# Batch 0's keys with heads on the partition groups, turned by VectorE; the sketch matrices loaded from two queues and converted by VectorE alone

## The chip, the core and the metric

One of the eight cores of a Trainium2 chip runs the whole program. Its engines work side by side: PE (TensorE, matmuls and full transposes, results into PSUM), DVE (VectorE), ACT (ScalarE), POOL (GpSimd) and SP, which here only issues transfers. ACT can issue transfers too. The metric is the device time of one execution in microseconds (us); lower is better.

## What is computed

Two blocks in a row. The first is an attention with a polynomial sketch: q, k, v are 4 batches x 4 heads x 1088 tokens x 32 channels, S1 and S2 are 8 x 32.

```python
def phi(x):                       # 32 channels -> 64 features
    a = einsum('rd,bhsd->bhsr', S1, x)
    b = einsum('rd,bhsd->bhsr', S2, x)
    return einsum('bhsi,bhsj->bhsij', a, b).reshape(..., 64)
q_p, k_p = phi(q), phi(k)
kv  = einsum('bhsf,bhsd->bhfd', k_p, v);  z = sum(k_p, axis=2)
x   = (q_p @ kv) / (q_p . z + 1e-6)       # -> 4352 tokens x 128
h   = x @ w_in                            # 128 -> 2048
out = gelu(h) @ w_out                     # exact gelu, 2048 -> 128
```

q, k and v are float32. S1, S2, w_in and w_out arrive as float64, and the kernel rounds them to float32 itself from their two 32-bit words.

## The kernel before, in words

The 1088 tokens of a batch are 8 x 128 in the "main" part and 64 "rem". For batch 0 everything before the first product with w_in is a chain that nothing else can cover: keys and values must be summed into kv before any query can be answered. The engines take their instructions in the order in which the program's text issues them (lines 1218 to 1224 chain them), and a transfer queue likewise, so the order of the text is the order of the work. From the first `hidden` step on (line 1164) the program is a long software pipeline of matmuls with w_in and w_out, into which the attention of later batches is slotted.

What happens ahead of that pipeline for batch 0, with the names in the code:

- Loads (lines 187 to 200). ACT issues S1 and S2, then loads its table of functions. SP issues the keys in two transfers of two heads (`load_main`, line 99: token p*8+j lies on partition p, all heads side by side), one transfer of queries, the values in two transfers, two remainders of keys and one of values, w_in's first piece, the second queries, w_in's second piece.
- PE runs products of zeros (`keep_busy`, line 887) until keys and sketches are there.
- The sketches are rounded by the class `Rounding` (line 243): DVE takes exponent and mantissa bits, ACT converts the low word (`low_words`) and the exponent (`exponents`), DVE joins them (`mantissas`, `signs`, `product_for_heads`).
- Keys: `key_turn(0, 0)` transposes four 128x128 blocks on PE into one PSUM bank and ACT copies them out (`kT`); `sketches` transposes the sketch matrix on PE, DVE makes `S12` (masked by head) and `sT`, POOL repeats `sT` into `Srep`; `key_turn_apart(0, 1)` transposes four more key blocks, ACT copies in two halves.
- `query_turn(0)`: DVE turns the first queries in 32x32 blocks. `widen_v`: POOL copies values next to a column of ones.
- `key_features` (line 387): 32 products of 64x32 per head pair on PE (`key_products`), an ACT copy of one half, a DVE product over all pairs of features (`k_p`); one of four such products goes to POOL.
- `expand_products(0)` repeats the queries' sketches on PE, ACT copies, DVE multiplies (`q_pT`).
- `kv_first` (line 420) sums k_p times v over tokens on PE for head pair r = 0 and 1, with the remainder (`key_turn_rem`, `key_features_rem`, `kv_first_rem`) in between; ACT takes the sum (`kz`, line 930).
- Then the first numerators, the division, two turns, and the first products with w_in (`first_hidden`, line 737).

Batches 1 to 3 already use another layout for their keys: `load_keys` (line 103) puts head h on partitions 32h to 32h+31, 32 consecutive tokens to a partition, and `key_turn_blocks` (line 365) turns them by a single DVE instruction per half, in 32x32 blocks.

Of the kernel before, what the change touches and what calls it, by code (L numbers as in the profile page):

```python
# [8 lines left out]
FP = mybir.dt.float32  # L9
U32 = mybir.dt.uint32  # L10
AX = mybir.AluOpType
# [5 lines left out]
def kernel(  # L17
# [19 lines left out]
    B, H, S, D = q.shape  # L37
    R = S1.shape[0]
    F = R * R
# [31 lines left out]
    def work_bank():  # L71
        return work_banks()[:, 0]
# [23 lines left out]
    raw = {}  # L96
    src_of = {"q": q, "k": k, "v": v}

    def load_main(eng, n, b, heads=slice(0, H)):
        eng.dma_start(out=main[n, b][:, heads],  # L100
                      in_=src_of[n][b, heads, 0:MAIN, :].rearrange("h (p j) d -> p h j d", j=J))

    def load_keys(b):

        for h in range(H):
            sp.dma_start(out=main["k", b][h * 32:(h + 1) * 32].rearrange("t x j d -> t (x j d)"),
                         in_=k[b, h, 0:MAIN, :].rearrange("(t n) d -> t (n d)", t=32))

    def load_values(b):

        src = v[b, :, 0:MAIN, :].rearrange("h (t q n) d -> q t h (n d)", t=32, q=4)
        for g in range(4):
            sp.dma_start(out=main["v", b][g * 32:(g + 1) * 32].rearrange("t h n d -> t h (n d)"), in_=src[g])
# [14 lines left out]
                sp.dma_start(out=q_rem[h * 32:(h + 1) * 32, b % 2, b // 2],  # L128
                             in_=q[b, h, MAIN:S, :].rearrange("(n t) d -> t n d", t=32))

    def load_rem(n, b):
        sp.dma_start(out=rem[n][b // 2 * REM:(b // 2 + 1) * REM, b % 2],
                     in_=src_of[n][b, :, MAIN:S, :].rearrange("h p d -> p h d"))

    half_block = []
# [48 lines left out]

    S_dst = landing(SR, S1.dtype != FP)

    for i, s in enumerate((S1, S2)):
        s, e = words(s)
        act.dma_start(out=S_dst[i * R:(i + 1) * R, :], in_=s)
    nc.scalar.preload_act_table_set("gelu_and_others")  # L190
    for r in range(2):
        load_main(sp, "k", 0, slice(r, H, 2))
    load_q(0)
    for r in range(2):
        load_main(sp, "v", 0, slice(r, H, 2))
    for n, b in (("k", 0), ("k", 2), ("v", 0)):
        load_rem(n, b)
    load_w_in(0)
    load_q(1)
    load_w_in(1)  # L200
# [42 lines left out]
    class Rounding:  # L243
# [15 lines left out]
            if self.wide:  # L259
                act.activation(out=self.low, in_=self.lo, func=ACT.Copy, scale=2.0 ** -52)  # L260

        def fields(self):
            self.exponent_fields()
            self.mantissa_fields()

        def exponent_fields(self):
# [50 lines left out]
    def sketches():  # L317
        ps = work_bank()
        pe.transpose(ps[:, :2 * R], in_=SR_heads.rearrange("r h d -> r (h d)"), identity=ident[:2 * R, :2 * R])
        dve.tensor_mul(out=S12, in0=ps[:, None, :2 * R].broadcast_to([128, H, 2 * R]),  # L320
                       in1=mask4[:, :, None].broadcast_to([128, H, 2 * R]))
        dve.tensor_copy(out=sT, in_=ps[:, :2 * R])
        for i in range(2):
            src = sT[:, 0:R, None] if i == 0 else sT[:, None, R:2 * R]
            pool.tensor_copy(out=Srep[:, i], in_=src.broadcast_to([128, R, R]))

    def transposed(ps, name, srcs, copy, midway=lambda: None):

        n = len(srcs) * 128
        for i, s in enumerate(srcs):  # L330
            if 2 * i == len(srcs):
                midway()
            pe.transpose(ps[:, i * 128:(i + 1) * 128], in_=s, identity=ident)  # L333
# [4 lines left out]
    def four_tokens(n, b, h, c):  # L338
        return main[n, b][:, h, c * JC:(c + 1) * JC, :].rearrange("p j d -> p (j d)")


    kT, k_p, k_p_rem = {}, {}, {}

    def widen_v(r):
# [5 lines left out]
        rows = slice(b // 2 * REM, (b // 2 + 1) * REM)  # L350
        pool.tensor_copy(out=v_rem_aug[b][rows, :, 0:D], in_=rem["v"][rows, b % 2])

    def key_turn(b, r, ps, copy, midway=lambda: None):
        kT[r] = transposed(ps, "kT", [four_tokens("k", b, h, c) for h in (r, r + 2) for c in range(NCH)], copy, midway)

    def key_turn_apart(b, r, banks, copy):

        kT[r] = att.tile([128, CW], FP, name="kT")
        for h, ps in zip((r, r + 2), banks):
            for c in range(NCH):  # L360
                pe.transpose(ps[:, c * 128:(c + 1) * 128], in_=four_tokens("k", b, h, c), identity=ident)
        for i, ps in enumerate(banks):
            copy(out=kT[r][:, i * 256:(i + 1) * 256], in_=ps[:, :256])

    def key_turn_blocks(b, x):

# [9 lines left out]
    def key_products(r, banks, col=0):  # L376

        for i in range(2 * NCH):
            for c in range(2):
                for t in range(2):  # L380
                    at = i * 128 + c * 64
                    pe.matmul(banks[t][c * 64:(c + 1) * 64, col + i * 32:col + (i + 1) * 32],
                              lhsT=kT[r][t * 64:(t + 1) * 64, at:at + 64],
                              rhs=S12[t * 64:(t + 1) * 64, 2 * t:2 * t + 2].rearrange("p h r -> p (h r)"),
                              start=True, stop=True)

    def key_features(b, r, banks, by_pool=()):
        key_products(r, banks)

        k_p[b, r] = att.tile([128, 2, J, R, R], FP, name="k_p")  # L390
        a = att.tile([128, 2, J, 2 * R], FP, name="a_t")
        for t in (1, 0) if by_pool else (0, 1):
            ab = banks[t][:, :128].rearrange("p (n r) -> p n r", r=2 * R)
            if t in by_pool:
                act.copy(out=a[:, t], in_=ab)
                pool.tensor_mul(**spread(k_p[b, r][:, t], a[:, t, :, 0:R], a[:, t, :, R:2 * R]))
            else:
                act.copy(out=a[:, t, :, 0:R], in_=ab[:, :, 0:R])
                dve.tensor_mul(**spread(k_p[b, r][:, t], a[:, t, :, 0:R], ab[:, :, R:2 * R]))

    def key_turn_rem(pair, ps, copy):

        kT["rem"] = transposed(ps[:, 256:], "kT_rem", [rem["k"][:, pair].rearrange("p h d -> p (h d)")], copy)

    def key_features_rem(pair, ps):

        for rows in (slice(0, 64), slice(64, 128)) if pair == 0 else (slice(0, 128),):
            pe.matmul(ps[rows, 384:448], lhsT=kT["rem"][:, rows], rhs=S12.rearrange("p h r -> p (h r)"), start=True, stop=True)
        k_p_rem[pair] = big.tile([128, H, R, R], FP, name=f"k_p_rem{pair}")
        ab = ps[:, 384:448].rearrange("p (h r) -> p h r", r=2 * R)  # L410
        a = att.tile([128, H, R], FP, name="a_rem")
        act.copy(out=a, in_=ab[:, :, 0:R])
        dve.tensor_mul(**spread(k_p_rem[pair], a, ab[:, :, R:2 * R]))

    k_s = {}

    def flat(features):
        return features.rearrange("p i j -> p (i j)")

    def kv_first(ps, r, tokens=range(J)):  # L420

        for i in tokens:

            ch, t, one = i // 4, i // 2 % 2, i % 2
            for c in range(NP):
                pe.matmul(ps[c * F:(c + 1) * F, r * 2 * D:r * 2 * D + C], lhsT=flat(k_p[0, r][:, t, c * 4 + ch * 2 + one]),  # L426
                          rhs=v_aug[r][:, c, i, :C], start=(r == 0 and i == 0), stop=False, skip_group_check=True)

    def kv_first_rem(ps):
# [457 lines left out]
    def keep_busy(n, ps, cols=256):  # L887
        for i in range(n):
            noughts = [nc.const_aps.tensor(0.0, [128, m], FP) for m in (128, cols)]
            pe.matmul(ps[:, CW - cols:], lhsT=noughts[0], rhs=noughts[1], start=True, stop=True)  # L890
# [2 lines left out]
    keep_busy(3, bank)  # L893
    keep_busy(1, bank, 64)
    r = Rounding(SR)
    r.low_words()
    r.fields()
    r.exponents()
    r.mantissas()
    r.signs()  # L900
    r.product_for_heads(SR_heads)
    key_turn(0, 0, hidden_bank(), by_act)
    keep_busy(1, bank, 128)
    sketches()
    key_turn_apart(0, 1, [hidden_bank(), work_bank()], by_act)
    query_turn(0)
    widen_v(0)
    banks = [out_bank(), out_bank()]
    key_features(0, 0, banks)
    key_features(0, 1, [hidden_bank(), hidden_bank()], by_pool=(1,))  # L910
    widen_v(1)
    widen_v_rem(0)
    expand_products(0)
    for i in range(2):
        query_features(0, i)
    kv_bank = out_bank()
    kv_first(kv_bank, 0, (0, 1, 4, 5))
    key_turn_rem(0, banks[1], by_act)
    kv_first(kv_bank, 0, (2, 3, 6, 7))
    key_features_rem(0, banks[1])  # L920
    kv_first(kv_bank, 1)
    kv_first_rem(kv_bank)
    w_in = [Rounding(w) for w in w_in_sb[:2]]
# [74 lines left out]
    def add_tokens(b):  # L998
# [11 lines left out]
    held = {}  # L1010

    def sketch_and_attend(n):

# [241 lines left out]
```

## Time and profile before

| | |
|---|---|
| median of 3 runs | 259.32 us (258.89 to 259.87) |
| span of the profiled execution, first to last instruction | 258.0 us (its own whole time isn't listed beside the span) |
| difference of the two | 1.3 us |
| PE busy | 253.9 us (98%) |
| DVE, ACT, POOL busy | 151.0, 115.5, 163.5 us |
| first product with w_in (L737) on the chain | starts at 15.45 us |
| granted TensorE clock | 1.000 |

Times in a view are counted from the span's start. A group line gives line, engine, operation, written tile <- read tiles, shapes and count. Where a timeline row merges several instructions, its first number is the start of the first, its second the time from there to the end of the last. Matmuls are pipelined and their ends are modelled, so PE can look busy where it is partly waiting for one product's end.

### The profile page before, as it was taken

How to read it: one execution, taken by the hardware profiler on the slowest of the kernel's cores; microseconds unless marked ns; L12 is line 12 of the kernel's file. 1: busy time of each engine (PE TensorE's matmuls, PEld its weight loads, DVE VectorE, ACT ScalarE, POOL GpSimd, SP SyncE). 2: the span in 40 equal slices, each digit the busy share in tenths (PEclk: the TensorE clock that was granted, in tenths of full speed). 3: DMA queues.
4: the chain of work that ended last, by engine and by line, in shares of the span. 5: the costliest groups of instructions: out<-in, count | busy, mean ns of one | idle time of the engine just before them, and what ended most of it. 6: DMA issues, size and time to landing. Idle time of an engine off the chain costs nothing.

```text
span 258.0 us, 5769 instructions
## 1 busy us (share of the span) xinstructions
PE 253.9 (98%) x2335; PEld 136.1 (53%) x2335; DVE 151.0 (59%) x312; ACT 115.5 (45%) x224; POOL 163.5 (63%) x173
## 2 busy tenths in 40 slices
PE   8999999999999999999999999999999999999995
PEld 7856444345444545544444455455444444445794
DVE  2786888969699997590187986399307000700330
ACT  4685777443626332443335332533444334433442
POOL 3403006799968788487758775787758777877300
PEclk9999999999999999999999999999999999999999
DMA  6469848721000101102000002000200200020020
GB/s 199 144 185 374 188 95 217 213 76 14 3 0 12 31 1 21 23 6 37 3 0 3 0 9 38 0 1 3 41 3 4 39 0 1 7 36 0 3 41 20
DMA packets 29594, 13.48 MB, mean 52 GB/s; under 512 B 21888, under 2 KB 27776, under 8 KB 29568
## 3 DMA queue, kind: packets, MB, share of 16 engines
q1 hardware_dynamic: 29392, 13.05, 20.3%
q8 instruction: 18, 0.29, 0.5%
q10 hardware_dynamic: 176, 0.07, 0.1%
q14 instruction: 8, 0.07, 0.1%
HBM read 10.88 MB, written 2.23 MB: 51 GB/s over the span
## 4 chain that ended last, share of the span: by engine, by line
PE 98%; DVE 1%; issue 0%; ACT 0%; DVEq 0%
PE h_ps L721 45%; PE o_ps L807 33%; PE o_ps L858 5%; PE w_ps L855 3%; PE w_ps L437 1%; PE w_ps L890 1%; PE w_ps L578 1%; PE w_ps L633 1%; PE o_ps L426 1%; PE h_ps L737 1%; PE w_ps L978 1%; PE w_ps L656 0%; PE w_ps L543 0%; DVE x_tok L679 0%; PE h_ps L333 0%; PE w_ps L333 0%
## 5 line engine op out<-in xcount | busy, mean ns | idle before, releaser
L721 PE MATMUL h_ps<-xT,w_in 128*64 128x512 f32 (+3 forms) x514 | 136.9, 576 | 0.0
L728 ACT ACTIVATE block<-h_ps 128x512 f32<-128x512 f32 (+1 forms) x128 | 73.0, 571 | 117.3 <-PE h_ps L721 115.3
L721 PEld LDWEIGHTS h_ps<-xT,w_in 128*64 128x64 f32 (+1 forms) x514 | 41.9, 143 | 30.4 <-issue 11.6
L807 PE MATMUL o_ps<-block,w_out 128*64 128x256 f32 x224 | 57.5, 379 | 0.0
L772 POOL TENSOR_TENSOR bits_low<-block 128x512 f32<-128x512 f32 x28 | 35.9, 1281 | 27.8 <-ACT block L728 27.8
L807 PEld LDWEIGHTS o_ps<-block,w_out 128*64 128x64 f32 x224 | 30.5, 137 | 38.0 <-issue 27.5
L773 POOL TENSOR_TENSOR bits_a<-block 128x512 f32<-128x512 f32 x28 | 35.7, 1277 | 12.0 <-ACT block L728 11.9
L822 DVE COPY sums<-o_ps 64x256 f32<-64x256 f32 x8 | 3.3, 416 | 60.6 <-PE o_ps L807 60.6
L774 POOL TENSOR_TENSOR bits_e<-bits_a,block 128x512 f32<-128x512 f32 x28 | 36.0, 1286 | 2.2
L775 POOL TENSOR_TENSOR bits_m<-block,bits_e 128x512 f32<-128x512 f32 x28 | 35.8, 1279 | 2.2
L807 PE MATMUL o_ps<-bits_low,small 128*64 128x256 f32 x112 | 28.8, 380 | 0.0
L807 PE MATMUL o_ps<-bits_a,small 128*64 128x256 f32 x112 | 28.8, 380 | 0.0
L807 PE MATMUL o_ps<-block,small 128*64 128x256 f32 x112 | 28.8, 379 | 0.0
L807 PE MATMUL o_ps<-bits_m,w_out 128*64 128x256 f32 x112 | 28.8, 380 | 0.0
L807 PEld LDWEIGHTS o_ps<-block,small 128*64 128x64 f32 x112 | 15.2, 137 | 17.9 <-issue 10.8
L807 PE MATMUL o_ps<-bits_e,small 128*64 128x256 f32 x112 | 17.1, 383 | 0.0
L858 PE MATMUL o_ps<-g,w_out 128*128 128x512 f32 (+1 forms) x34 | 16.5, 572 | 0.0
L807 PEld LDWEIGHTS o_ps<-bits_m,w_out 128*64 128x64 f32 x112 | 15.4, 137 | 0.0
L807 PEld LDWEIGHTS o_ps<-bits_a,small 128*64 128x64 f32 x112 | 15.2, 137 | 0.0
L807 PEld LDWEIGHTS o_ps<-bits_low,small 128*64 128x64 f32 x112 | 15.2, 137 | 0.0
L590 DVE STREAM_TRANSPOSE w_ps<-w_ps 128x512 f32<-128x512 f32 (+1 forms) x7 | 4.8, 687 | 17.1 <-ACT xT L644 12.7
L807 PEld LDWEIGHTS o_ps<-bits_e,small 128*64 128x64 f32 x112 | 7.7, 137 | 10.6 <-issue 8.8
(194 smaller groups left out, 305.1 us busy)
## 6 DMA issues: line engine op xcount, KB each, us to landing
block<-in_moe_w_in_dram SPq DMA_DIRECT2D x3, 512.0 KB, 8.4
block<-in_moe_w_out_dram SPq DMA_DIRECT2D x3, 512.0 KB, 12.1
k<-in_k_dram SPq DMA_DIRECT2D x12, 128.0 KB, 3.1
v<-in_v_dram SPq DMA_DIRECT2D x12, 128.0 KB, 3.4
q<-in_q_dram SPq DMA_DIRECT2D x24, 64.0 KB, 2.4
out_dram<-oT SPq DMA_DIRECT2D x21, 64.0 KB, 2.2
k<-in_k_dram SPq DMA_DIRECT2D x2, 256.0 KB, 2.8
q<-in_q_dram SPq DMA_DIRECT2D x2, 256.0 KB, 3.9
```

Source lines behind the costliest of these rows:

```text
L426: pe.matmul(ps[c * F:(c + 1) * F, r * 2 * D:r * 2 * D + C], lhsT=flat(k_p[0, r][:, t, c * 4 + ch * 2 + one]), rhs=v_aug[r][:, c, i, :C], s ...
L590: dve.transpose(out=tok, in_=ps[:, :, :H2])
L721: pe.matmul(ps[rows, :W], lhsT=w[:, rows], rhs=xT[n][:, :W], start=True, stop=True)
L728: act.activation(out=g_of[n, fi][:, :W], in_=ps[:, :W], func=ACT.Gelu)
L772: pool.tensor_sub(out=s[3], in0=a11, in1=a21)
L773: pool.tensor_add(out=s[1], in0=a21, in1=a22)
L774: pool.tensor_sub(out=s[2], in0=s[1], in1=a11)
L775: pool.tensor_sub(out=s[4], in0=a12, in1=s[2])
L807: pe.matmul(acc[n][bank][half * 64:(half + 1) * 64, col:col + HW], lhsT=fixed, rhs=moving, start=opens and e == 0 and name in "4715", stop ...
L822: dve.tensor_copy(out=N[lo, 0, one], in_=a0[lo, one])
L855: pe.matmul(o_of[n][i][:, :128], lhsT=g[:, i * 128:(i + 1) * 128], rhs=w_tile(w_out_sb, fi), start=first, stop=final)
L858: pe.matmul(o_of[n][:, cols], lhsT=w_tile(w_out_sb, fi), rhs=g[:, cols], start=first, stop=final)
```

## The change

Batch 0's keys are loaded as those of the other batches: head h on partitions 32h to 32h+31. Heads 2 and 3 are issued by ACT, heads 0 and 1 by SP. S2 is the first transfer on SP, S1 stays the first on ACT. The two key remainders move to ACT's queue, behind its table load. The values are loaded in four transfers instead of two, 32 partitions each. The loads of w_in and of the second queries stay on SP in their order.

On the engines: the eight key transposes on PE and the three copies by ACT go. DVE turns the keys instead, by two instructions of 128x512 (`key_turn_first`). Both turns now come behind the sketches. The sketches' conversion runs on DVE alone: `fields(by_dve=True)` replaces the two ACT activations by three DVE instructions. `sT` is copied by ACT instead of DVE. The key products are as many as before (`key_products_first`), grouped by half of the tokens (x) instead of by head pair (r), so `kv_first` over the first four tokens needs half x = 0 of both banks, and over the last four half x = 1. `query_turn(0)` stands behind the first of the four feature products instead of ahead of them; POOL still makes one of these four products, between its two copies of values. One product of zeros of 256 columns stands behind the sketches, one of 128 behind the key products.

```diff
+    def load_keys(b, queue=sp, heads=range(H)):
+        for h in heads:
+            queue.dma_start(out=main["k", b][h * 32:(h + 1) * 32].rearrange("t x j d -> t (x j d)"),
+                            in_=k[b, h, 0:MAIN, :].rearrange("(t n) d -> t (n d)", t=32))
...
-    for i, s in enumerate((S1, S2)):
+    for i, (queue, s) in enumerate(((act, S1), (sp, S2))):
         s, e = words(s)
-        act.dma_start(out=S_dst[i * R:(i + 1) * R, :], in_=s)
+        queue.dma_start(out=S_dst[i * R:(i + 1) * R, :], in_=s)
+    load_keys(0, act, range(2, H))
     nc.scalar.preload_act_table_set("gelu_and_others")
-    for r in range(2):
-        load_main(sp, "k", 0, slice(r, H, 2))
+    for b in (0, 2):
+        load_rem("k", b, act)
+    load_keys(0, sp, range(2))
     load_q(0)
-    for r in range(2):
-        load_main(sp, "v", 0, slice(r, H, 2))
-    for n, b in (("k", 0), ("k", 2), ("v", 0)):
-        load_rem(n, b)
+    load_values(0)
+    load_rem("v", 0)
...
+            if by_dve and self.wide:
+                dve.tensor_scalar(out=self.m, in0=self.e, scalar1=2.0 ** 23, scalar2=-896.0 * 2.0 ** 23, op0=AX.mult,
+                                  op1=AX.add)
+                dve.tensor_scalar(out=self.r, in0=self.m, scalar1=0.0, scalar2=None, op0=AX.max)
+                dve.tensor_scalar(out=self.low, in0=self.lo, scalar1=2.0 ** -52, scalar2=None, op0=AX.mult)
...
-        dve.tensor_copy(out=sT, in_=ps[:, :2 * R])
+        act.copy(out=sT, in_=ps[:, :2 * R])
...
+    def key_turn_first(x):
+        kT[x] = att.tile([128, CW], FP, name="kT")
+        dve.transpose(out=kT[x].rearrange("p (j q t) -> p q j t", q=4, j=4),
+                      in_=main["k", 0].rearrange("p q j d -> p q (j d)")[:, :, x * 128:(x + 1) * 128].rearrange("p q (j d) -> p q j d", d=D))
...
+    def key_products_first(x, banks):
+        for t in range(2):
+            for j in range(4):
+                for c in range(2):
+                    at = x * 128 + j * 32
+                    pe.matmul(banks[t][c * 64:(c + 1) * 64, at:at + 32],
+                              lhsT=kT[x][t * 64:(t + 1) * 64, j * 128 + c * 64:j * 128 + (c + 1) * 64],
+                              rhs=S12[t * 64:(t + 1) * 64, 2 * t:2 * t + 2].rearrange("p h r -> p (h r)"),
+                              start=True, stop=True)
...
     keep_busy(3, bank)
     keep_busy(1, bank, 64)
     r = Rounding(SR)
-    r.low_words()
-    r.fields()
-    r.exponents()
+    r.fields(by_dve=True)
     r.mantissas()
     r.signs()
     r.product_for_heads(SR_heads)
-    key_turn(0, 0, hidden_bank(), by_act)
+    sketches()
+    keep_busy(1, bank)
+    banks = [hidden_bank(), hidden_bank()]
+    for x in range(2):
+        key_turn_first(x)
+    for x in range(2):
+        key_products_first(x, banks)
     keep_busy(1, bank, 128)
-    sketches()
-    key_turn_apart(0, 1, [hidden_bank(), work_bank()], by_act)
+    key_features_first(0, 0, banks[0])
     query_turn(0)
     widen_v(0)
-    banks = [out_bank(), out_bank()]
-    key_features(0, 0, banks)
-    key_features(0, 1, [hidden_bank(), hidden_bank()], by_pool=(1,))
+    key_features_first(0, 1, banks[1])
+    key_features_first(1, 1, banks[1], by_pool=True)
+    key_features_first(1, 0, banks[0])
     widen_v(1)
     widen_v_rem(0)
     expand_products(0)
...
-    kv_first(kv_bank, 0, (0, 1, 4, 5))
-    key_turn_rem(0, banks[1], by_act)
-    kv_first(kv_bank, 0, (2, 3, 6, 7))
-    key_features_rem(0, banks[1])
+    kv_first(kv_bank, 0, range(4))
+    key_turn_rem(0, rem_bank, by_act)
+    kv_first(kv_bank, 0, range(4, J))
+    key_features_rem(0, rem_bank)
     kv_first(kv_bank, 1)
     kv_first_rem(kv_bank)
```

More of the change, by code (lines that the diff above doesn't have):

```diff
@@ L97 @@
     src_of = {"q": q, "k": k, "v": v}
[L99 to L107, printed above, removed]
+    def load_keys(b, queue=sp, heads=range(H)):
+        for h in heads:
+            queue.dma_start(out=main["k", b][h * 32:(h + 1) * 32].rearrange("t x j d -> t (x j d)"),
+                            in_=k[b, h, 0:MAIN, :].rearrange("(t n) d -> t (n d)", t=32))
     def load_values(b):
@@ L129, in load_q_rem, with load_rem @@
                              in_=q[b, h, MAIN:S, :].rearrange("(n t) d -> t n d", t=32))
-    def load_rem(n, b):
-        sp.dma_start(out=rem[n][b // 2 * REM:(b // 2 + 1) * REM, b % 2],
+    def load_rem(n, b, queue=sp):
+        queue.dma_start(out=rem[n][b // 2 * REM:(b // 2 + 1) * REM, b % 2],
                      in_=src_of[n][b, :, MAIN:S, :].rearrange("h p d -> p h d"))
@@ L260, in low_words, with fields @@
                 act.activation(out=self.low, in_=self.lo, func=ACT.Copy, scale=2.0 ** -52)
-        def fields(self):
+        def fields(self, by_dve=False):
             self.exponent_fields()
+            if by_dve and self.wide:
[3 more added lines that the diff above has]
+                dve.tensor_scalar(out=self.low, in0=self.lo, scalar1=2.0 ** -52, scalar2=None, op0=AX.mult)
             self.mantissa_fields()
@@ L336, in transposed @@
         return t
-    def four_tokens(n, b, h, c):
-        return main[n, b][:, h, c * JC:(c + 1) * JC, :].rearrange("p j d -> p (j d)")
     kT, k_p, k_p_rem = {}, {}, {}
@@ L351, in widen_v_rem @@
         pool.tensor_copy(out=v_rem_aug[b][rows, :, 0:D], in_=rem["v"][rows, b % 2])
[L353 to L363, printed above, removed]
+    def key_turn_first(x):
+        kT[x] = att.tile([128, CW], FP, name="kT")
+        dve.transpose(out=kT[x].rearrange("p (j q t) -> p q j t", q=4, j=4),
+                      in_=main["k", 0].rearrange("p q j d -> p q (j d)")[:, :, x * 128:(x + 1) * 128].rearrange("p q (j d) -> p q j d", d=D))
     def key_turn_blocks(b, x):
@@ L374, in spread, with key_features_first @@
                     in1=b[:, :, None, :].broadcast_to([128, n, R, R]))
[L376 to L383, printed above, removed]
+    def key_products_first(x, banks):
[5 more added lines that the diff above has]
+                              lhsT=kT[x][t * 64:(t + 1) * 64, j * 128 + c * 64:j * 128 + (c + 1) * 64],
                               rhs=S12[t * 64:(t + 1) * 64, 2 * t:2 * t + 2].rearrange("p h r -> p (h r)"),
                               start=True, stop=True)
[L387 to L399, printed above, removed]
+        k_p[0, x] = att.tile([128, NP, J, R, R], FP, name="k_p")
+        held["a", x] = att.tile([128, NP, J, 2 * R], FP, name="a_t")
+    def key_features_first(x, t, ps, by_pool=False):
+        a, ab = held["a", x], ps[:, x * 128:(x + 1) * 128].rearrange("p (n r) -> p n r", r=2 * R)
+        if by_pool:
+            act.copy(out=a[:, t], in_=ab)
+            pool.tensor_mul(**spread(k_p[0, x][:, t], a[:, t, :, 0:R], a[:, t, :, R:2 * R]))
+        else:
+            act.copy(out=a[:, t, :, 0:R], in_=ab[:, :, 0:R])
+            dve.tensor_mul(**spread(k_p[0, x][:, t], a[:, t, :, 0:R], ab[:, :, R:2 * R]))
     def key_turn_rem(pair, ps, copy):
@@ L413, in key_features_rem @@
         dve.tensor_mul(**spread(k_p_rem[pair], a, ab[:, :, R:2 * R]))
-    k_s = {}
+    k_s, held = {}, {}
     def flat(features):
@@ L422, in kv_first @@
         for i in tokens:
-            ch, t, one = i // 4, i // 2 % 2, i % 2
             for c in range(NP):
-                pe.matmul(ps[c * F:(c + 1) * F, r * 2 * D:r * 2 * D + C], lhsT=flat(k_p[0, r][:, t, c * 4 + ch * 2 + one]),
+                pe.matmul(ps[c * F:(c + 1) * F, r * 2 * D:r * 2 * D + C], lhsT=flat(k_p[0, i // 4][:, c, i % 4 * 2 + r]),
                           rhs=v_aug[r][:, c, i, :C], start=(r == 0 and i == 0), stop=False, skip_group_check=True)
@@ L915 @@
         query_features(0, i)
-    kv_bank = out_bank()
-    kv_first(kv_bank, 0, (0, 1, 4, 5))
-    key_turn_rem(0, banks[1], by_act)
-    kv_first(kv_bank, 0, (2, 3, 6, 7))
-    key_features_rem(0, banks[1])
+    kv_bank, rem_bank = out_bank(), out_bank()
+    kv_first(kv_bank, 0, range(4))
+    key_turn_rem(0, rem_bank, by_act)
+    kv_first(kv_bank, 0, range(4, J))
+    key_features_rem(0, rem_bank)
     kv_first(kv_bank, 1)
@@ L1008, in add_tokens @@
         dve.tensor_add(out=to[rows], in0=sums[rows], in1=k_p_rem[b % 2][rows].rearrange("p (c r) i j -> p c (r i j)", c=NP))
-    held = {}
     def sketch_and_attend(n):
```

## The prediction

> **What bounds the kernel now.** The chain of waits comes first. PE holds 98% of it, and from 15.45 us on there is nothing in it but products; so a change in the opening is worth what it does to the start of that first product with w_in, one to one. Its shares, from the page, and its first pieces (start, us, what):
>
> ```profile
> PE 98%; DVE 1%; issue 0%; ACT 0%; DVEq 0%
> ```
>
> ```profile
> 0.77 3.22 PE w_ps L890 x8
> 4.00 0.85 PE h_ps L333 x4
> ...
> 6.54 0.78 PE o_ps L382 x32
> 7.32 0.47 PE h_ps L382 x32
> 7.78 1.05 PE w_ps L543 x32
> 8.83 0.59 PE o_ps L426 x16
> ...
> 10.50 0.91 PE o_ps L426 x32
> 11.41 0.35 PE o_ps L432 x8
> ...
> 15.45 1.06 PE h_ps L737 x8
> ```
>
> Two times matter: 8.83, where `kv_first` starts right behind `expand_products` (L543), and 11.76 (11.41 + 0.35), where kv is complete. Between them PE takes 2.93 us without a break.
>
> Second, the timeline of the same stretch shows who feeds PE (start, length, instruction):
>
> ```profile
> 3.63 0.17 DVE L268 TENSOR_SCALAR bits_e<-raw_SR 16x32 uint32<-16x32 uint32 x1 [2.67 <-DMA raw_SR<-in_S_dram]
> 4.46 0.28 DVE L302 TENSOR_TENSOR SR_heads<-bits_m,bits_e 16x128 f32<-16x128 f32 x1
> 5.21 0.28 PE L319 MATMUL w_ps<-ident,SR_heads 16*128 16x16 f32 x1
> 5.60 0.22 DVE L320 TENSOR_TENSOR S<-w_ps,mask 128x64 f32<-128x64 f32 x1 [0.86 <-PE w_ps L319]
> 5.92 0.71 DVE L528 STREAM_TRANSPOSE qT<-q 128x512 f32<-128x512 f32 x1
> 6.68 0.61 POOL L345 COPY sums<-v 128x512 f32<-128x512 f32 x1 [0.31 <-DMA v<-in_v_dram]
> 7.62 1.29 DVE L399 TENSOR_TENSOR k_p<-a_t,o_ps 128x512 f32<-128x512 f32 x2 [0.99 <-ACT a_t L398]
> 8.23 1.06 POOL L396 TENSOR_TENSOR k_p<-a_t 128x512 f32<-128x512 f32 x1 [0.94 <-ACT a_t L395]
> 9.24 0.61 POOL L345 COPY sums<-v 128x512 f32<-128x512 f32 x1
> 9.79 0.29 POOL L351 COPY v_rem_aug<-v_rem 64x128 f32<-64x128 f32 x1
> ```
>
> DVE has slack: it waits 0.86 and 0.99 us. PE has none, and spends part of it on key transposes. The sketches are ready at 4.74 (4.46 + 0.28), but PE reaches their transpose only at 5.21.
>
> Third, the groups by shape of 0 to 16 us: the same 128x128 transpose at about 4 us and at 11.7 us.
>
> ```profile
> L333 PE MATMUL h_ps<-ident,k 128*128 128x128 f32 x4 | 1.1, 421 | 0.0
> L333 PE MATMUL w_ps<-ident,q 128*128 128x128 f32 x4 | 0.7, 286 | 0.0
> ```
>
> 421 ns against 286: PE runs slow at first, though the granted clock reads 1.00 in every row. Counts in windows of 0.1 us put the step at about 6.65 us (6 products of L382 a window before 6.6, 17 to 22 after 6.9).
>
> **The change part by part.** The sum is against the profiled execution: span 258.0, 1.3 under the median of 259.32.
>
> *Sketches.* S2 is issued by ACT at 1.38 and lands at 3.62, 1.95 after its issue ended at 1.67. Now SP issues it at 0.73; with 0.45 per issue (row of the keys' loads) it lands near 3.1, and S1, whose issue ends at 1.35, near 3.3. Bounds: 2.4 (0.74 plus 1.7, the landing of the 8 KB q_rem transfers) and 3.6 (no gain). I take 3.2, from S2's own row. The conversion goes from 1.11 us (3.63 to 4.74) to eight DVE instructions in a line: 0.17 + 0.17 + 0.17 + 0.17 + 0.16 + 0.18 + 0.18 + 0.28 = 1.48, less some overlap where nothing depends: 1.4. So they are ready at 4.6 instead of 4.74. PE now transposes them at once; from PE's start to `S12` is 0.39 in the row, so `S12` runs 5.05 to 5.25 instead of 5.60 to 5.82: a gain of 0.55. `sT` on ACT costs the chain nothing: `Srep` needs 0.41 on POOL and is used after 8 us.
>
> *Keys.* Eight PE transposes (1.90 on the chain with their waits) and three ACT copies (0.58, 0.37, 0.37) go. In their place two DVE turns of 0.67 to 0.71 (rows L368, L528) follow `S12`: 5.2 to 6.6. They need all four key transfers. Before, 512 KB flowed by 3.65 and were there by 4.0. Two now go out behind S2 on SP, two behind S1 on ACT, the last by about 2.1; 2.7 from issue to landing (the row's least) gives 4.8, in time by 0.4. Upper bound 5.2 (3.1, the later 128 KB loads): still in time. The rearranged access of the new turn is not in the trace; bounds 0.67 and twice that, and I take 0.70 because the rows agree for any source so far. Products: half 0 from 5.95, half 1 from 6.65, done by 7.4 (0.85 and 0.65 as in the rows), against 7.78.
>
> *DVE's line.* Here the gain goes. Before, the queries' turn stood at 5.92, in DVE's idle time. Now the first feature product (0.65) and then the turn (0.70) follow the key turns: 6.7 to 7.35, and 8.05. `expand_products` waits for that turn: it starts at 8.1 instead of 7.78 and ends at 9.2 instead of 8.83. The other two feature products end at 8.7 and 9.35; `q_pT` waits for ACT's copy (0.59) as before and ends near 11.1 instead of 10.78, of which DVE's 0.54 of idle time before the denominators hides part. PE is 0.35 later.
>
> *Transfers.* SP's issues sum to about the same (S2 and two more value loads in, two remainders of 0.61 and 0.76 out). But a transfer waits for an earlier one to land once eight are in flight: in the built program the second value load waits for a key transfer of head 2, the third for head 3, the fourth for head 0. So three value loads go out at about 4.5 to 5.9, instead of 2.3 to 3.4 for both halves. A 128 KB value load lands in 2.4 (least) to 3.4 (median): 7.8 to 8.8; I take 8.2 as the queue is short then. w_in's first piece leaves near 6.5 instead of 5.49, the second queries near 7.0 instead of 6.14, w_in's second piece near 7.5 instead of 6.61. At 3.8 us each they land by 11.3, and are used at 10.63, 11.69 and 12.86: 10.3 for the first leaves 0.3. These I cost at nothing; without that slack each tenth would be one of the end. The key remainders leave ACT after its table load, near 3.6 to 4.9, and are used at 9.35; `sT` and the first `a_t` copy queue behind them on ACT, which is free by 5.
>
> *POOL's line.* The first copy of values waits for all four loads: 8.2 to 8.8 (before 6.68). Behind it wait the feature product (1.06, to 9.9), the second copy (10.5) and the remainder's (10.8). The second half of `kv_first`'s first round, due at 9.2 + 0.59 + 0.26 = 10.05, needs the product at 9.9: just in time. PE then ends kv at 12.15 instead of 11.76.
>
> *Sum:* 0.55 gained at the sketches and 0.38 at the products, none of which reaches PE's next stage, which starts 0.35 to 0.4 late: span 258.4, median 259.7.
>
> A rule against the change: the page "TensorE: Matmul & The Clock Gate" of the Trainium skill (Part 1, The HAM clock gate) says that the clock is halved until a free-running window of 3.4 us was busy. The trace agrees that it rises late, 5.9 us after the first product. By that page a window of the new opening that isn't busy enough would put the rise off by another 3.4 us, and the sum would be the first rival's 260.7; without it, it stands at 259.7.
>
> **The rivals.**
>
> - PE stays slow for longer (slower). Before, PE has work without a break from 0.77 to the step at 6.65. Now it stands idle about 4.0 to 4.6 for the sketches, 5.6 to 5.9 for the first key turn and 7.9 to 8.1 for the queries. For: PE was busy for 2.5 of the first 3.2 us and that did not bring the step. Against: two products of zeros fill most of the rest. While slow, the 1.05 of `expand_products` take twice as long, and the 2.93 of kv too. A step at 10 instead of 6.65 costs half of 8.1 to 10, 0.95, on top of 0.4: 260.7. It decides the sign of the verdict from a step at about 10 on. Range 260.3 to 262.
> - The values come late (slower). kv can't end before their landing plus 3.8 (0.61 + 1.06 + 0.59 + 0.23 + 0.91 + 0.35 and waits). At 9.2 instead of 8.2 that is 13.0, 1.2 late: 260.5. For: three loads wait for key landings. Against: little else is in flight then.
> - The rearranged turn takes twice 0.7: 1.4 later, 261.1. Against it speak six turns at 0.67 from another layout.
> - The sketches land at 2.4, the values at 7.6 (faster). `S12` is then bound by the zeros that end at 4.0, and kv ends at 11.4: 258.9. The 3.8 behind the values keeps it from being more.
>
> **How the numbers follow.** Likeliest, 0.45: PE's next stage 0.4 late, 259.7. Slow PE 0.25, late values 0.10, slow turn 0.05, early landing 0.15. A measurement of this kernel can tell about 0.5%, 1.3 us, from no change: 258.0 to 260.6. The likeliest case and the early landing lie within it; of the slow PE two thirds lie above it, of late values half, and the slow turn all, with some 0.05 from the likeliest case and the early landing running over: slower 0.32. Nothing worked out here reaches 258.0, so faster has 0.06, for what I have not seen. The range runs from 258.8, the early landing, to 261.2, two thirds into the slow PE.
>
> **What would show it.** Right: `S12` near 5.1, two turns of 0.7 behind it, PE waiting for the queries' turn near 8.1, kv complete near 12.1, w_in's products as before behind it. Wrong: transposes at 421 ns beyond 8 us; POOL's first copy of values after 9; a wait for w_in's pieces; or the queries' turn before 7.5, with which the opening would be shorter.

## The result, and the profile after

The changed kernel takes 267.16 us (266.37 to 267.63) against 259.31 us before: 1.029 times as long, with an interval of 1.028 to 1.031. The prediction was 259.7 us, with a range up to 261.2. PE's clock, which makes most of the difference, was on its list as a rise that comes late, with a chance of 0.25 and a price of 1 us. It cost about 5, and in the profiled run it was a fall.

The profiled run of the changed kernel took 266.37 us, with a span of 264.6: 6.6 longer than the span before. Two rows of its page, in 40 slices of 6.6 us each (PE's busy share and the granted TensorE clock, in tenths), and the shares of its chain of waits:

```profile
PE   6999999999999999999999999999999999999994
PEclk9559999999999999999999999999999999999999
...
PE 96%; DMA 1%; DVE 1%; ACTq 0%; ACT 0%; issue 0%; DVEq 0%
```

The two fives in the clock's row are new. In the second and third slice PE is busy nine tenths and more, at half speed. The windows of PE show where that begins and ends (columns: stretch, its length, PE's busy time and number of products, granted clock, DMA share, GB/s):

```profile
3.57:6.98 3.41, 2.07 (x54) 1.00 1.05 245
...
5.00:5.20 0.20, 0.00 (x0) 1.00 1.02 312
...
6.80:7.00 0.20, 0.20 (x22) 0.95 1.02 227
7.00:7.20 0.20, 0.20 (x18) 0.50 1.00 192
...
6.98:10.39 3.41, 2.88 (x52) 0.50 0.94 255
10.39:13.80 3.41, 3.41 (x57) 0.50 0.06 20
13.80:17.21 3.41, 3.41 (x58) 0.50 0.00 0
17.21:20.62 3.41, 3.41 (x95) 0.50 0.70 194
```

The clock falls at 6.98 and comes back at 20.62, 13.64 us later. That is four times 3.41, which is why the long stretches are cut in that length. In the stretch ahead of the fall PE was busy for 2.07 of 3.41, 61%; in the last three of the four slow ones it had no break at all.

It had been up before. The trace's own list of clock changes begins with a rise at 3.57, and the two zeros at 4.18 take 0.70, where the same two take 1.22 in a run below whose clock is first up at 13.54. In the kernel before, the first rise is listed at 6.91. So in this run the clock came up earlier than before, stayed up for one stretch of 3.41 and fell again.

The chain of waits up to the first product with w_in:

```profile
1.73 3.33 DMA k<-in_k_dram
5.26 0.72 DVE kT L353
6.02 1.41 PE h_ps L373 x54
7.70 0.69 DVE k_p L388
8.39 0.63 DVE qT L516
9.15 2.01 PE w_ps L531 x32
11.17 1.00 PE o_ps L414 x16
...
15.92 1.05 PE w_ps L334 x4
...
21.69 1.13 PE h_ps L725 x8
```

Set against the pieces shown of before, `expand_products` starts at 9.15 instead of 7.78, 1.37 later, and takes 2.01 instead of 1.05. The four transposes of the second queries (L334, 15.92) take 1.05 instead of the 0.59 that the chain before has for them at 11.76. The first product with w_in starts at 21.69 instead of 15.45, 6.24 later. Of that, 1.37 has come by the start of `expand_products`; the other 4.87 come between there and the first product (12.54 instead of 7.67), where PE's work is the same in number and shape and has no wait before it that it did not have. Behind 21.69 nothing more of size is lost.

Who feeds PE is seen in the timeline (start, length, instruction, and in brackets how long the engine had stood idle and for whom):

```profile
2.33 0.36 DVE L269 TENSOR_SCALAR bits_e<-raw_SR 16x32 uint32<-16x32 uint32 x1 [1.38 <-DMA raw_SR<-in_S_dram]
3.62 0.28 DVE L303 TENSOR_TENSOR SR_heads<-bits_m,bits_e 16x128 f32<-16x128 f32 x1
4.18 0.70 PE L878 MATMUL w_ps<-const-float32-0.0 128*128 128x256 f32 x2
5.26 1.31 DVE L353 STREAM_TRANSPOSE kT<-k 128x512 f32<-128x512 f32 x2 [0.68 <-DMA k<-in_k_dram]
6.02 1.88 PE L373 MATMUL h_ps<-S,kT 64*64 64x32 f32 x64 [1.15 <-DVE kT L353]
7.45 0.21 ACT L387 COPY a_t<-h_ps 128x64 f32<-128x64 f32 x1 [2.67 <-PE h_ps L373]
7.70 0.69 DVE L388 TENSOR_TENSOR k_p<-a_t,h_ps 128x512 f32<-128x512 f32 x1 [1.14 <-ACT a_t L387]
8.30 0.70 DVE L516 STREAM_TRANSPOSE qT<-q 128x512 f32<-128x512 f32 x1
8.92 0.61 POOL L342 COPY sums<-v 128x512 f32<-128x512 f32 x1 [3.66 <-DMA v<-in_v_dram]
9.15 2.01 PE L531 MATMUL w_ps<-qT,Srep 32*64 32x256 f32 x32 [0.53 <-DVE qT L516]
```

PE stands idle from 4.88 to 6.02, since the keys are there only at 5.26 and then have to go through DVE. Before, PE had no break here: zeros, the sketches' transpose and the key transposes that the change takes away follow one another from 4.00 to 6.54.

So the first theory: the idle place lets the clock fall, and the small products behind it don't bring it back. Its rival: the opening is simply longer, by the waits in the timeline (keys, the copy of `a_t`, the queries' turn, the values), and the slow products only fill time that something else sets.

### The profile page after: what moved, and what is told of

It is laid out like the page before. It is cut to its first block, busy times and chain, and to the rows that moved or that the text cites. A ratio compares the mean times of both kernels' runs of the same rounds, so it can differ in the third digit from the quotient of the medians.

```text
span 264.6 us, 5757 instructions
## 1 busy us (share of the span) xinstructions
PE 258.2 (98%) x2329; PEld 138.7 (52%) x2329; DVE 152.7 (58%) x316; ACT 113.9 (43%) x220; POOL 164.1 (62%) x173
## 4 chain that ended last, share of the span: by engine, by line
PE 96%; DMA 1%; DVE 1%; ACTq 0%; ACT 0%; issue 0%; DVEq 0%
PE h_ps L709 44%; PE o_ps L795 32%; PE o_ps L846 5%; PE w_ps L843 3%; PE w_ps L531 1%; PE w_ps L425 1%; PE o_ps L414 1%; PE w_ps L566 1%; PE w_ps L621 1%; DMA k<-in_k_dram 1%; PE h_ps L725 1%; PE w_ps L969 1%; PE h_ps L373 1%; PE w_ps L334 0%; PE w_ps L644 0%; PE h_ps L644 0%
```

## Experiments

Each kernel was timed beside the kernel before on the same chip; the medians of before lay between 259.3 and 259.5.

**Both idle places filled.** Products of zeros are added where PE stands idle; nothing else changes, so all waits stay.

```diff
     sketches()
-    keep_busy(1, bank)
+    keep_busy(3, bank)
...
-    keep_busy(1, bank, 128)
+    keep_busy(3, bank)
     key_features_first(0, 0, banks[0])
```

> The changed kernel with more products of zeros in PE's two idle places: three of 256 columns instead of one behind the sketches (the keys come at 6.0 us, PE sat idle from 4.88), and three of 256 columns instead of one of 128 behind the key products. Theory C (clock): the changed kernel lost 4.9 of its 6.6 us because PE's clock stood at half from 7.0 to 20.6 us, after a stretch from 3.6 to 7.0 in which PE had little to do; with the stretch filled the clock stays up, the granted clock reads 1.00 past 8 us with 128x128 transposes at 286 ns, and the time falls to 261 to 262.5 us. Theory W (waits): the time went to keys, queries and values that come later and to the new order, and the slow clock only stretches idle time; then more zeros can only delay PE, and the time stays at 267 us or above.

Measured: 261.67 us (261.26 to 261.89), 1.0074 [1.0052, 1.0095] times the kernel before. Five and a half of the lost microseconds come back for more work on PE. The granted clock reads 1.00 in all slices; the list of clock changes has a rise at 4.11 and no fall before 260.11. Its chain:

```profile
9.11 1.15 PE w_ps L531 x32
10.26 0.59 PE o_ps L414 x16
```

`expand_products` starts at 9.11, as late as in the changed kernel (9.15), and takes 1.15 instead of 2.01. From there to the first product with w_in, at 16.81, it is 7.70; before it was 7.67. The groups by shape of the opening say the same of single products. First the changed kernel's, then those of this run:

```profile
L531 PE MATMUL w_ps<-qT,Srep 32*64 32x256 f32 x64 | 4.0, 641 | 0.5 <-DVE qT L516 0.5
L414 PE MATMUL o_ps<-sums,k_p 128*64 128x33 f32 x64 | 4.0, 295 | 0.0
L334 PE MATMUL w_ps<-ident,q 128*128 128x128 f32 x4 | 1.1, 434 | 0.0
```

```profile
L531 PE MATMUL w_ps<-qT,Srep 32*64 32x256 f32 x64 | 2.3, 386 | 0.0
L414 PE MATMUL o_ps<-sums,k_p 128*64 128x33 f32 x64 | 2.4, 223 | 0.0
L334 PE MATMUL w_ps<-ident,q 128*128 128x128 f32 x4 | 0.7, 286 | 0.0
```

So the rival fails for the larger part: with the same waits the clock alone is worth 4.84 (12.54 less 7.70). The 1.33 by which `expand_products` still starts late (9.11 less 7.78) is left, and the waits have to explain only that.

**One place at a time.** The same fill in the first place alone, behind the sketches (the first hunk above), and in the second alone, behind the key products (the second hunk).

> The changed kernel with more products of zeros in the first idle place alone: three of 256 columns instead of one behind the sketches; behind the key products one of 128 as in the change. Theory C1: the idle 1.1 us ahead of the key products (4.9 to 6.0 us) is what brings the clock down, so filling it alone keeps the clock up: 261 to 262.5 us, as with both places filled. Theory C2: any idle PE in the opening does it, and the one ahead of the queries' products (8.6 to 9.1 at the slow clock, 7.8 to 9.1 at the full one) as well: 263 to 267 us, with the slow clock in the records past 10 us.

Measured: 261.59 us (261.47 to 261.72), 1.0079 [1.0052, 1.0105], with the clock at 1.00 throughout. The first place is enough.

> The changed kernel with more products of zeros in the second idle place alone: three of 256 columns instead of one of 128 behind the key products; behind the sketches one of 256 as in the change. Theory C1: the first idle place is left as it was, so the clock is down at 7 us as in the change; the zeros then take 2.6 us at the slow clock (to about 10), and they and the queries' products may bring the clock up near 10.4 us, or not before 14: 264 to 268 us. Theory C2: filling either place helps about equally: 262 to 264 us.

Measured: 263.79 us (262.88 to 264.87), 1.0164 [1.0114, 1.0214]: less slow than the first theory expected. The number lies in the range of the second, but either place does not help alike, since the first alone gives 261.59. The runs fall into two groups, 262.88 and 262.98 with a mean clock of 0.992, 264.61 and 264.87 with one of 1.00. The profiled run, of 264.87 us, has this chain:

```profile
6.40 2.45 PE h_ps L373 x64
8.85 2.86 PE w_ps L878 x6
11.70 2.00 PE w_ps L531 x32
13.70 0.59 PE o_ps L414 x16
```

The clock is down here: the zeros themselves take 2.86, nearly twice the 1.50 of the same six in the run with both places filled, and `expand_products` behind them takes 2.00. The list of clock changes has the first rise at 13.54, so in this run the clock was not up at all before. From 13.70 on the sums run at 0.59, while in the changed kernel they run at 1.00 from 11.17 to the end. The 3.41 ahead of the rise hold zeros up to 11.70 and `expand_products` from there; which of them brought the clock up is not shown. The 3.41 before those, full as well, with key products and 1.3 of zeros, ended without a rise.

**How full is full enough.** Two products of zeros behind the sketches instead of three or one.

```diff
     sketches()
-    keep_busy(1, bank)
+    keep_busy(2, bank)
```

> The changed kernel with two products of zeros of 256 columns behind the sketches instead of one (three kept the clock up); behind the key products one of 128 as in the change. Theory C1, by the share of a window: PE idles some 0.7 us ahead of the key products instead of 1.15. If what counts is how much of a window of about 3.4 us is filled, and the limit lies between one and three products, the runs fall into two groups, near 261.6 us (clock up) and near 265 to 267.5 us (clock down), by where the window begins. Rival: any idle place ahead of the key products brings the clock down; then all runs lie at 265 us or above.

Measured: 261.53, 261.38, 261.44 and once 266.45 us; two groups, as the first theory expected, and the last run has a mean clock of 0.974, as the profiled run of the changed kernel has. With the clock up the ratio is 1.0081 [1.0052, 1.0109]. One product of zeros was too little in all four runs of the changed kernel (266.4 to 267.6), two were enough in three of four, three in all fifteen runs of the two kernels above that have them there, and in all 26 of the four kernels below (at most 262.34).

The profiled run, of 261.53 us, has the clock up from 4.04 on. Two stretches of 3.41 behind that rise, in the same view as above, and a row of its timeline:

```profile
4.04:7.45 3.41, 2.53 (x67) 1.00 1.07 246
7.45:10.86 3.41, 2.35 (x61) 1.00 0.81 241
...
9.18 1.12 PE L531 MATMUL w_ps<-qT,Srep 32*64 32x256 f32 x32 [1.06 <-DVE qT L516]
```

In the second of them PE stands idle for 1.06 without a break, nearly the 1.15 of the changed kernel, and the clock stays up. So the length of one idle place doesn't decide alone. This stretch was busy to 69%, the one ahead of the fall in the changed kernel to 61%; whether the busy share is what counts, and where the limit lies, two such stretches can't show.

**Does the kernel before need its zeros as well?** Its five products of zeros are left out; the rest is as before.

```diff
     bank = work_bank()
-    keep_busy(3, bank)
-    keep_busy(1, bank, 64)
...
-    keep_busy(1, bank, 128)
     sketches()
```

> The kernel before without any product of zeros (five matmuls less, nothing else changed). Theory C: PE's first work is then the key transposes near 4 us, the clock rises at least one window of 3.4 us later and perhaps not before the dense products at 15 us, so the opening takes 3 to 6 us longer: 262 to 265 us. Theory W: nothing waits for those products, so the time stays at 259.3 us (within 0.5).

Measured: 260.56, 265.5, 264.9 and 266.23 us. Three of four runs lose 5 to 7 us, as the change does, with no key moved; the 19 runs of the kernel before beside them lie between 258.68 and 261.89. The fourth, which is the profiled one, has the key transposes and products running from 3.40 without a break, `expand_products` slow (1.94 from 7.63) and the sums nearly at speed from 9.57 (0.68). The list of clock changes has the rise at 9.74; the 3.41 ahead of it hold key products and `expand_products`. The other three were not traced; their time suggests that the clock came up later there. The kernel before, too, loses this time in most runs when its zeros are gone.

**Parts of the change alone.** First the sketches: S2 first on SP, the conversion by DVE, `sT` by ACT, in the kernel before.

```diff
-    for i, s in enumerate((S1, S2)):
+    for i, (queue, s) in enumerate(((act, S1), (sp, S2))):
...
-    r.low_words()
-    r.fields()
-    r.exponents()
+    r.fields(by_dve=True)
```

> The kernel before with the sketches' part of the change alone: S2 issued by SP, conversion on VectorE alone, sT copied by ACT; keys, values and queries as before. Theory C: PE's work stays as dense as before, so the clock rises as before and the time is 259.0 to 259.4 us, same. Theory W: the sketches land about 1.2 us earlier, but PE reaches them at 5.2 us in its order, so also same; a clearly slower run would put the loss into the sketches' part and would speak against both.

Measured: 259.48 us (259.26 to 261.44), 1.0008 [0.9979, 1.0037]. `expand_products` starts at 7.08, 0.6 earlier than before (7.71 in the same view), and yet the first product with w_in starts at 15.44 (before 15.45). The chain tells why:

```profile
5.86 0.60 SPq L173
6.46 0.04 issue
6.50 5.07 DMA q<-in_q_dram
```

The second queries, the last but one of the opening's loads on SP, land at 11.57, and their turn on PE follows at 11.71, against 11.76 before. A shorter opening runs into them.

Then the rest of the change, the keys with the values' loads and the new order, with the sketches as before (both issued by ACT, ACT in the conversion, `sT` by DVE):

```diff
-    for i, (queue, s) in enumerate(((act, S1), (sp, S2))):
+    for i, (queue, s) in enumerate(((act, S1), (act, S2))):
...
-        act.copy(out=sT, in_=ps[:, :2 * R])
+        dve.tensor_copy(out=sT, in_=ps[:, :2 * R])
...
-    r.fields(by_dve=True)
+    r.low_words()
+    r.fields()
+    r.exponents()
```

> The changed kernel with the sketches as before: both issued by ACT, low word and exponent converted by ACT, sT copied by VectorE; keys by heads on partition groups and turned by VectorE. Theory C: it is the keys' part that takes PE's work out of the opening, so the loss stays: 266 to 268.5 us, with the slow clock in the records or from the start. Theory W: the sketches are ready some 0.5 to 1 us later than in the changed kernel and the keys wait for them, so 267.5 to 268.5 us.

Measured: 268.78 us (268.61 to 269.07), 1.0346 [1.0295, 1.0398]. The loss comes with this part, and the sketches' part of the change saves 1.6 of it. The clock is up at 4.20 here and falls at 7.61, behind 3.41 in which PE was busy for only 0.84, and stays down for 17.07, five times 3.41. The keys are turned at 6.83 instead of 5.26, because the two that ACT issues, now behind both sketches, take 4.6 to land, against 2.5 for the two that SP issues; in the changed kernel it is 3.0 for either pair. In the view of the transfers issued up to 3.2 us (count, size, median us from issue to landing):

```profile
k<-in_k_dram SPq DMA_DIRECT2D x2, 128.0 KB, 2.5
...
k<-in_k_dram ACTq DMA_DIRECT2D x2, 128.0 KB, 4.6
```

**The waits that are left.** With the first place filled, the queries' turn goes ahead of the first feature product, and the zeros behind the key products go.

```diff
-    keep_busy(1, bank)
+    keep_busy(3, bank)
...
-    keep_busy(1, bank, 128)
-    key_features_first(0, 0, banks[0])
     query_turn(0)
+    key_features_first(0, 0, banks[0])
```

> The changed kernel with the first idle place filled (three products of zeros of 256 columns), the products of zeros behind the key products taken out, and the queries' turn on VectorE ahead of the first feature product instead of behind it. Theory Q: what is left of the loss with the clock up (261.7 against 259.5 us) is that the queries' products start at 9.1 instead of 7.8 us, because their turn stands behind a feature product that waits for the key products. Then they start near 7.7 us and the time is 259.5 to 260.5 us. Theory V: the values land at 8.8 us instead of 6.7, and what waits for them on GpSimd ends kv at 13.1 us anyway: 261 to 261.7 us.

Measured: 261.21 us (260.94 to 261.42), 1.0064 [1.0045, 1.0083]. `expand_products` starts at 7.68, as early as before the change (7.71 in the same view), but only 0.5 of the 1.4 gained there reaches the first product with w_in (16.30). The timeline shows what is late next:

```profile
7.68 1.12 PE L531 MATMUL w_ps<-qT,Srep 32*64 32x256 f32 x32
8.69 0.61 POOL L342 COPY sums<-v 128x512 f32<-128x512 f32 x1 [3.38 <-DMA v<-in_v_dram]
9.36 0.66 PE L414 MATMUL o_ps<-sums,k_p 128*64 128x33 f32 x16 [0.56 <-POOL sums L342]
```

PE stands idle for the values. They land at about 8.5 with the changed order of loads, and POOL's copy of them, which had been covered by the late `expand_products`, is now what the sums wait for.

Two more runs try to move the values. In the first, each half of the key products gets PSUM banks of its own, and the key remainders go back to SP, behind the values:

```diff
-    for b in (0, 2):
-        load_rem("k", b, act)
...
     load_values(0)
+    for b in (0, 2):
+        load_rem("k", b)
...
-    banks = [hidden_bank(), hidden_bank()]
+    banks, banks1 = [out_bank(), out_bank()], [hidden_bank(), hidden_bank()]
...
-        key_products_first(x, banks)
+        key_products_first(x, (banks, banks1)[x])
```

> As the kernel with the queries' turn ahead, and besides: the two key remainders back on SP behind the values (so the second to fourth value load no longer wait for key transfers to land, or only the last), and the key products of each half in PSUM banks of their own, so that ScalarE's first copy doesn't wait for the second half. Theory Q: little is left to gain by this, 259.3 to 260.3 us, and no faster than the kernel with the queries ahead by more than 0.3. Theory V: the values then land near 7.9 us, and this is the step that brings the time down: 0.7 to 1.2 us faster than that kernel, to about 259.5 to 260.5 us.

Measured: 260.96 us (260.65 to 261.35), 1.0047 [1.0019, 1.0075]. The copy of `a_t` now starts 0.70 after the first key product (7.36 against 6.66), where it was 1.29 in the run with the queries first, with the clock up as well (7.53 against 6.24): it waits for one half only. POOL's copy of the values comes at 8.53 and the sums at 9.20, a little earlier, but the second queries, issued behind the remainders, now set the chain: their turn on PE starts at 12.69, and the first product with w_in at 16.41.

The second adds to this that ACT issues half of the values, and that the value remainder goes behind the second queries:

```diff
+    load_values(0, act, range(2, 4))
     load_keys(0, sp, range(2))
     load_q(0)
-    load_values(0)
+    load_values(0, sp, range(2))
...
-    load_rem("v", 0)
     load_w_in(0)
     load_q(1)
+    load_rem("v", 0)
```

> As the kernel with the queries' turn ahead, the first idle place filled and the key products in banks of their own (261.0 us), and besides the values' four loads issued two by ACT behind its table load and two by SP, so that only the last waits for a key transfer; the key remainders follow on SP, the values' remainder goes behind the second queries. Theory V: what is left of the loss is the values, copied by GpSimd from 8.5 us on instead of 6.7; they now land 0.5 to 1 us earlier, kv is complete near 11.7 us, and the time is 259.9 to 260.6 us. Theory D: VectorE's line (two key turns, the queries' turn, three feature products, done at 9.5 us) holds kv back by itself, and the time stays at 260.8 to 261.2 us.

Measured: 260.75 us (260.73 to 260.83), 1.0055 [1.0038, 1.0072], the first product with w_in at 16.12. The second queries are no longer late, but the values are as late as ever, although all four loads left earlier (2.34 to 4.21, against 2.49 to 5.30 in the run with the queries first):

```profile
8.69 0.62 POOL L343 COPY sums<-v 128x512 f32<-128x512 f32 x1 [3.37 <-DMA v<-in_v_dram]
```

The last of them, in the chain of the run with the queries first and then of this one (start, us):

```profile
5.30 3.19 DMA v<-in_v_dram
```

```profile
4.21 4.27 DMA v<-in_v_dram
```

It leaves 1.09 earlier and lands at the same 8.48 or 8.49. The prediction had the wait of the value loads for key loads as a reason for late values; here leaving earlier did not bring the last load in earlier.

One more run asks whether it is the split over two queues that brings the keys so late: all four go out on SP.

```diff
-    load_keys(0, act, range(2, H))
...
-    load_keys(0, sp, range(2))
+    load_keys(0, sp)
```

> The kernel with the first idle place filled and the queries' turn ahead, with all four key transfers on SP, ahead of queries and values, instead of two on SP and two on ACT. Theory S (sharing): with keys on ACT and queries and values on SP, the second queue's transfers run beside the keys and take half the engines; on one queue the keys go first. Then the last key transfer, though issued 0.7 us later (near 2.5), lands by about 4.8 to 5.1 instead of 5.4, the key turn starts there, and the time is within 0.5 us of the 261.2 of that kernel or better. Theory I (issue): the landing follows the issue, so the keys land near 5.8 to 6.0 and the time is 261.5 to 262 us.

Measured: 261.32 us (261.08 to 262.34), 1.0085 [1.0058, 1.0112], beside 261.21 for the same kernel with the keys on two queues. The keys are turned at 5.59, between the two expectations. Each load takes less (2.7 us in the median, against 2.9 for SP's and 3.1 for those of ACT on two queues), but the last one leaves later, at 2.49. The time lies in the range of the first theory, the turn does not; neither theory of the landing is shown by this.

None of these versions is faster than the kernel before; the best, at 260.75, is still 0.55% slower.

## Why the prediction was wrong

- **The clock: the step that failed.** The sum took PE's products at the durations that they have before, with one rise of the clock near 6.65 (6.91 in the trace's list) and no fall, and priced a later rise as a rival: "A step at 10 instead of 6.65 costs half of 8.1 to 10, 0.95". In the profiled run the clock rose at 3.57, fell at 6.98 and was back only at 20.62, and the cost was 4.87 (or 4.84 between two runs that differ by zeros alone). So the rival named the right part, but not its course: a fall behind a rise was not among the rivals. Two more things in this step were wrong. "Two products of zeros fill most of the rest" against the rival: the one behind the sketches took 0.70 of a place that lasts from 4.18 to 6.02. And the rival took it for granted that a clock that is down rises at the end of the next full stretch. In the trace two of them, busy from end to end, ended with the clock still at 0.50, and only the end of the third brought it up. With that the rival's range ended at 262. The sign that the prediction named for a slow PE came, a transpose of 421 ns beyond 8 us: at 15.92 it is 434.
- **What I had from the skill.** The page "TensorE: Matmul & The Clock Gate" of the Trainium skill (Part 1, The HAM clock gate) has a free-running window of 3.4 us. The trace agrees: 13.64 us of slow clock are four of 3.41, and the fall lies at the end of one that was busy to 61%. It has the clock come up after one busy window; here it did not after two full ones of small products, at 10.39 to 17.21, and "another 3.4 us", as I had it by that page, was too little.
- **Sketches.** Forecast to land at 3.2; they were there at 2.33, just under the lower bound of 2.4. The conversion took 1.57 (2.33 to 3.90), forecast 1.4. So the gain at this step was larger than my 0.55, and of no use: the keys were not there.
- **Keys.** Forecast to be there at 4.8, upper bound 5.2. The turn began at 5.26, released by the last key transfer. I called the upper bound "still in time", which held only beside my own late sketches. The two turns took 0.72 and 0.6 (1.31 together), as forecast, so the rival of a slow turn is out.
- **Key features.** Forecast at 6.7, came at 7.70. I let the first copy follow the products of the first half. It came only behind those of both halves, which share a bank; with banks of their own (the run with four banks) it follows the first half. With the late keys that makes 1.0 that the sum does not have.
- **The queries' turn.** That it would make `expand_products` wait was right, with the turn at 8.3 (forecast 7.35) and PE at 9.15 (forecast 8.1), later by the missing 1.0. This is the second term that was too small: `expand_products` was put 0.35 to 0.4 late and is 1.37 late. With the clock up and nothing else changed it is 1.33, and the time of 261.6 to 261.7 still lies above the range.
- **Values.** Forecast at 8.2, came at 8.92 in POOL's row. So late values were there too, but hidden behind the late `expand_products`. It shows only where that comes earlier (0.56 of PE's idle time in the run with the queries first).
- **Later transfers at nothing.** Right for the changed kernel: neither w_in nor the second queries are on its chain. The sketches alone and the four banks show how thin the cover is: the second queries become the chain as soon as `expand_products` starts 0.6 earlier.
- **Behind the opening.** Right: from the first product with w_in on, the delay stays as it is, 6.24 there and 6.6 at the end of the span.

The sum of what was measured against the profiled runs: 1.37 of waits, 4.87 of clock, 0.4 behind 21.69 that I have not traced: 6.6 of span. A comparison of medians gives 7.85, since the profiled run of the changed kernel is the fastest of its four and its span is 1.8 below its time, while in the base of the prediction I had 1.3 for that difference. In other runs of the kernel before it is 1.8 as well, so the profiled execution of before was some 0.5 longer than its median. The two runs of the changed kernel at 267.6 us have a mean clock of 1.000, so no fall is on record for them. That fits a clock that first came up late, as the rival had it: the record counts as 1.00 what lies ahead of the first rise, and the profiled run with the second place filled reads 0.999 although its clock is first up at 13.54. For the runs at 267.6 this is argued from their time and mean, not traced.

Left open: why POOL can copy the values only at 8.5 to 8.9 in most of these orders of loads (at 9.10 with the sketches as before, at 9.32 with all keys on SP), also where ACT issues half of them, while the DMA engines are close to fully used from 2.5 to 9 us (a share of 0.82 to 1.17 in the changed kernel); and what in PE's work raises the clock or leaves it down. The full stretches that ended without a rise in the changed kernel hold mostly sums; the four traced rises that come late (9.74 without zeros, 13.54 with the second place filled, 20.62 in the changed kernel, 24.68 with the sketches as before) each end a stretch with 1.7 to 2.0 of `expand_products` in it. But in the last of these runs a stretch with 2.0 of it, busy to 91%, ended without a rise.

## What to carry to other kernels

Work taken off PE in a stretch where the clock is not yet safely up has to be priced by what the clock then does to everything behind it, and not only by the wait: here a stretch with an idle place of 1.15 us cost 4.9. When a change empties PE, put products of zeros into the hole and see how many it takes over several runs, as here two products were enough in three runs of four and three in all. A mean clock of 1.00 doesn't tell that the clock was up in the opening; the length of a known product does. And before moving transfers, look at which one is next in line on the chain: a gain of 0.6 at the start of an opening was lost to the second queries, and 1.4 shrank to 0.5 by the values.

## What the runs showed of the hardware

- The granted clock stayed at 0.50 through 10.2 us of unbroken small products (10.39 to 20.62 in the changed kernel). The same products run at full speed, without losing the clock, where it was up ahead of them (0.59 for a round of sums in the runs with filled places, 1.00 here). So it depends on the past.
- The views read a clock of 1.00 ahead of the first rise that the trace lists, while the products there are slow: the same two zeros behind the sketches took 1.22 in the run with the second place filled (first rise at 13.54) and 0.70 in the changed kernel (first rise at 3.57), both under a clock of 1.00.
- The first rise came at another time in each traced run, though all kernels but the one without zeros open with the same zeros from 0.77 to about 4.0: at 6.91 before, at 3.57 in the changed kernel, at 4.11 with both places filled, at 13.54 with the second. One run of a kernel says little about it.
- A 128 KB load of keys issued by ACT took 4.6 us in one order of loads and 3.0 in another, those of SP 2.5 and 3.0 in the same two (medians of two loads each).
